# RWKV-7 attention into a SoLU block: where layer norm's mean is taken out, and a new order of the first pieces

## The chip, the cores and the metric

The kernel runs on one core of a Trainium2 chip. A core has five engines that run beside each other, each with its own stream of instructions: TensorE (PE in the profile, with its weight loads as PEld), VectorE (DVE), ScalarE (ACT), GpSimd (POOL) and SyncE (SP, which here only issues DMAs). Each engine executes its stream in the order in which the program emitted it and waits on semaphores of the others. The metric is the time of one execution on the device, in microseconds; lower is better.

## The reference

The first half is a recurrence over 768 time steps for 4 batches and 8 heads of width 40; its answers, 3072 tokens of 320 values, go into a block with a soft-max-weighted activation and a layer norm:

```python
for t in range(S):
    y[:, :, t] = np.einsum('bhd,bhde->bhe', rt, state)
    Sa = np.einsum('bhde,bhe->bhd', state, at)
    state = state * wt - outer(Sa, bt) + outer(vt, kt)
...
h = x @ w_in                                  # 3072 x 320 by 320 x 1024
e = np.exp(h - max(h));  solu = h * e / sum(e)
ln = (solu - mean(solu)) / sqrt(var(solu) + 1e-6) * g_ln
out = ln @ w_out                              # 1024 x 320
```

The weights `w_in` and `w_out` arrive as 64-bit floats, which the kernel narrows to 32 bits itself, in 13 pieces.

## The kernel before

**Chunks and slots.** Time is cut into 12 chunks of 64 steps; a piece of work called chunk i is one such chunk of two batches, so there are N = 24 of them, in two independent chains that take turns. The recurrence inside a chunk is solved with a triangular inverse of 32x32 blocks, one inversion for two chunks, in 30 dependent steps on VectorE (pieces `i0.1` to `i11.30`). The main loop runs over slots i. A slot solves chunk i of the recurrence (`S`, `R1`, `an`), prepares chunk i+1 (scores `Sk`, `Sv`, couplings `C` and `D` with their ScalarE copies `wy` and `tl`, state `Sr` with its copy `Esr`, and `K`, which reads that state), begins chunk i+5 (`w`, `a`, `b`, `k` loads, `Tc`, `Ta`, `Tb`, `N`) and runs the layer block of chunk c = i-2: the five products `H` of x with w_in, the maximum `m`, the exponential `e`, the weighing `we`, the spread `sq` with its power `rs`, then one slot later the turning `Te` with its copy `Ee`, and the products `P` and `Pr` with w_out, their scaling `Eo` and the store `So`.

**The layer norm before.** `we` (line 878, VectorE) multiplies e with h in place and gives its mean `mu`. `sq` (lines 889 to 891, ScalarE) is three instructions: the small `c2`, one pass over 128x1024 that squares (mu - 1024 e) into PSUM with a running sum, and the small `var`. `rs` (line 899, GpSimd) raises var to the power -1/2. The products with w_out use e without its mean taken out. Instead, each row of w_out (already scaled by g_ln) has the mean over all 1024 rows subtracted once, at the start: `mean_part` and `mean_more` (lines 284 and 288) build that mean with TensorE in three parts (pieces `Tmean0`, `Tmean1`, `Tmean2` in slots 1, 2 and 3), `mean_kept` (line 294) copies it with ScalarE, and `centred` (line 299, piece `centre`) subtracts it from w_out with two VectorE instructions of 128x1280. The first product `P0` reads w_out after that.

**Order.** Every piece is recorded under its name in the order of the loops, then all are emitted sorted by their place in the string `ORDER`. Names that are not in the string follow in the order of the loops. The string holds the pieces up to about slot 10, so from slot 11 on the order is the one that the loop's code gives. DMAs are issued by the engine whose queue they are given: most by SP, some loads, the inversions' blocks and x by POOL. They stand in that engine's order like its other instructions.

**Splits.** A product `H` is four matmuls of 64x512, each of which the table `SPLITS` can cut into two of 256 columns; each appears twice in the profile, since a 32-bit product takes two passes.

Of the kernel before, what the change touches and what calls it, by code (L numbers as in the profile page):

```python
# [9 lines left out]
FP32 = mybir.dt.float32  # L10
# [17 lines left out]
SPLITS = {2: (0, 0, 0, 2, 4), 24: (0, 0, 0, 0, 2)}  # L28
# [7 lines left out]
lg3 Tc3 xi3 k1 sb2 i0.1 i0.2 i0.3 i0.4 i0.5 i0.6 Tb2 Eb2 i0.7 i0.8 xe3 Tei3 Eei3 i0.9 i0.10 i0.11 i0.12 w4 N2 nt2 a3  # L36
Ta3 b3 b4 b5 i0.13 i0.14 w5 lg4 Tc4 xi4 xe4 sb3 Tb3 i0.15 i0.16 sn2 i0.17 i0.18 Tk0 cv0 Tv0 Ekv0 Tei4 K0 Ea3 Eb3 N3 a4
i0.19 L2 i0.20 i0.21 i0.22 i0.23 i0.24 i0.25 sb4 i0.26 i0.27 lg5 cr0 Tr0 nt3 Er0 i0.28 L3 Tc5 xe5 i0.29 i0.30 Eei4 sn3
a5 Tei5 Ta4 Ea4 v1 nb2 nb3 r1 ns3 Sv0 Sk0 mk0 mv0 V0 ns2 cv1 sk1 Eei5 nf3 nf2 B1 i1.1 i1.2 i1.3 x0.0 Ta5 xi5 sb5 Tb4
i1.4 i1.5 i1.6 i1.7 U0 i1.8 i1.9 i1.10 i1.11 cr1 Tv1 r2 Eb4 L4 nb4 Tk1 Ekv1 Tr1 Er1 cr2 Sk1 mk1 tu0 F0 N4 nt4 k2 i1.12  # L40
i1.13 i1.14 C0 sk2 g ns4 K1 wy0 i1.15 i1.16 uh0 i1.17 i1.18 D0 tu1 Sv1 mv1 w6 tl0 S0 lg6 Tc6 F1 Ea5 mlu0 V1 i1.19
i1.20 i1.21 k3 sk3 i1.22 i1.23 uh1 xi6 xe6 L5 nb5 clu0 R0.0 R1.0 an0 Tb5 Eb5 x0.1 Tei6 Eei6 Tg ks0 a7 v2 a6 Ta6 L6 L7
w7 Eg Tr2 N5 cv2 Tv2 Er2 b6 nt5 L8 i1.24 i1.25 i1.26 i1.27 i1.28 Tk2 Ekv2 i1.29 i1.30 lv0 C1 wy1 Sv2 ns5 D1 tl1 Ea6
nf4 nb6 Sk2 mk2 mv2 Ts2 sn5 S1 mlu1 nf5 nb7 Z2 lg7 Tc7 Es2 Sr2 ns6 Esr2 R0.1 K2 nf6 U1 xi7 sb6 clu1 nb8 R1.1 an1 sn4
l0 H0.0 ks1 ns7 nf7 xe7 Tei7 ns8 nf8 b7 Tb6 Eb6 Eei7 Ta7 Ea7 r3 cr3 B2 i2.1 i2.2 i2.3 i2.4 H0.1 i2.5 i2.6 i2.7 i2.8 V2
x0.2 H0.2 H0.3 i2.9 Tr3 Er3 uh2 N6 nt6 Ts3 Es3 Tmean0 Emean0 k4 Sr3 tu2 F2 C2 sk4 v3 cv3 w8 lg8 L11 L9 L10 H0.4 wy2
Esr3 D2 tl2 Tk3 w9 Tv3 i2.10 i2.11 i2.12 lv1 i2.13 sb7 Ekv3 Tc8 xe8 xi8 i2.14 Sv3 nb9 m0 i2.15 tu3 Tei8 b8 ns9 nf9 Tb7
# [33 lines left out]
def shape_constants():  # L81
# [19 lines left out]
def kernel(  # L101
# [1329 lines left out]
```

## Time and profile before

| | us |
|---|---|
| median of three runs | 529.92 (528.12 to 532.23) |
| the profiled execution | 526.91 |
| its span | 525.0 |
| TensorE busy | 479.6 (91%) |
| VectorE busy | 419.1 (80%) |
| ScalarE busy | 320.4 (61%) |
| GpSimd busy | 182.9 (35%) |

The span is what the profiler shows from the first instruction to the last; the execution's own time is 1.9 us longer. Everything that is worked out below is added to the profiled execution's 526.91 us and then moved to the median. A share of busy time is a mean over the start, where weights are narrowed and the first inversions run, the steady slots, and the end, where nothing is left but the layer block.

### The profile page before, as it was taken

How to read it: one execution, taken by the hardware profiler on the slowest of the kernel's cores; microseconds unless marked ns; L12 is line 12 of the kernel's file. 1: busy time of each engine (PE TensorE's matmuls, PEld its weight loads, DVE VectorE, ACT ScalarE, POOL GpSimd, SP SyncE). 2: the span in 40 equal slices, each digit the busy share in tenths (PEclk: the TensorE clock that was granted, in tenths of full speed). 3: DMA queues.
4: the chain of work that ended last, by engine and by line, in shares of the span. 5: the costliest groups of instructions: out<-in, count | busy, mean ns of one | idle time of the engine just before them, and what ended most of it. 6: DMA issues, size and time to landing. Idle time of an engine off the chain costs nothing.

```text
span 525.0 us, 28146 instructions
## 1 busy us (share of the span) xinstructions
PE 479.6 (91%) x12029; PEld 340.8 (65%) x12029; DVE 419.1 (80%) x1800; ACT 320.4 (61%) x651; POOL 182.9 (35%) x328
## 2 busy tenths in 40 slices
PE   4557587898999999999999999999999999999996
PEld 3345574766667776767776777776676767666544
DVE  5599989998998999878789879979989798443321
ACT  4646476785676654755766676666666656665433
POOL 3533246243434342543152433434252521211200
PEclk9999999999999999999999999999999999999999
DMA  9997869756666777686175675676654542421211
GB/s 161 177 187 141 181 111 217 160 119 128 140 123 142 127 164 129 149 168 135 30 147 112 114 150 119 117 150 129 126 116 90 117 111 67 96 53 28 75 41 26
DMA packets 201772, 63.97 MB, mean 122 GB/s; under 512 B 173368, under 2 KB 194592, under 8 KB 201648
## 3 DMA queue, kind: packets, MB, share of 16 engines
q1 hardware_dynamic: 188528, 41.61, 43.3%
q0 software_dynamic: 10768, 19.95, 15.5%
q8 instruction: 95, 1.56, 1.2%
q10 hardware_dynamic: 2352, 0.62, 0.6%
q14 instruction: 29, 0.24, 0.2%
HBM read 47.96 MB, written 14.16 MB: 118 GB/s over the span
## 4 chain that ended last, share of the span: by engine, by line
PE 73%; DVE 10%; DMA 6%; ACT 4%; SPq 3%; issue 3%; DVEq 0%; ACTq 0%
PE po L320 18%; PE h L320 18%; PE pyo L320 6%; PE px L320 6%; PE py L320 5%; PE ps L320 4%; PE pu L320 3%; DVE prod L562 2%; DVE uu L565 2%; PE plnT L911 2%; SPq L346 2%; PE pkv L437 2%; PE psr L320 2%; PE pa L437 2%; PE pb L437 2%
## 5 line engine op out<-in xcount | busy, mean ns | idle before, releaser
L320 PE MATMUL h<-w_in,xT 64*64 64x512 f32 (+1 forms) x1064 | 121.2, 552 | 1.7 <-issue 1.2
L320 PE MATMUL po<-w,lnT 128*64 128x320 f32 (+1 forms) x768 | 112.2, 432 | 0.0
L562 DVE TENSOR_TENSOR prod<-blk,uu 128x48 f32<-128x48 f32 (+19 forms) x576 | 93.5, 203 | 1.2
L565 DVE TENSOR_TENSOR uu<-uu,prod 128x48 f32<-128x48 f32 (+19 forms) x576 | 93.9, 203 | 0.0
L527 POOL DMA_DIRECT2D nt_dram<-nt x86 | 50.2, 591 | 101.9 <-ACT nt L515 100.7
L320 PEld LDWEIGHTS po<-w,lnT 128*64 128x64 f32 (+1 forms) x768 | 53.9, 139 | 41.6 <-issue 1.1
L320 PEld LDWEIGHTS h<-w_in,xT 64*64 64x64 f32 x1064 | 41.7, 133 | 31.4 <-issue 27.7
L899 POOL TENSOR_TENSOR rs<-var,mhalf 128x1 f32<-128x1 f32 x24 | 16.5, 686 | 120.4 <-ACT var L891 120.1
L862 DVE TENSOR_REDUCE nmax<-h 128x1 f32<-128x1024 f32 x24 | 29.3, 1220 | 31.7 <-PE h L320 31.6
L346 POOL DMA_DIRECT2D raw_r<-in_r_dram x48 | 33.2, 696 | 23.5 <-ACT r L381 22.2
L890 ACT ACTIVATE sq<-e,mu 128x1024 f32<-128x1024 f32 x24 | 26.9, 1120 | 21.4 <-DVE e L878 21.4
L870 ACT ACTIVATE e<-h,nmax 128x1024 f32<-128x1024 f32 x24 | 26.7, 1112 | 19.4 <-DVE nmax L862 19.2
L481 DVE TENSOR_TENSOR lu<-pu,cst 128x512 f32<-128x512 f32 x24 | 16.5, 686 | 24.2 <-PE pu L320 24.2
L878 DVE SCALAR_TENSOR_TENSOR e<-h,e 128x1024 f32<-128x1024 f32 x24 | 29.3, 1219 | 5.8 <-ACT e L870 5.7
L641 ACT COPY tu<-py 32x256 f32<-32x256 f32 (+1 forms) x36 | 13.2, 365 | 30.4 <-PE py L320 30.2
L830 POOL DMA_DIRECT2D x_dram<-x x24 | 18.0, 751 | 36.4 <-DVE x L821 36.3
L693 ACT COPY st<-psr 128x416 f32<-128x416 f32 (+1 forms) x44 | 14.3, 378 | 24.6 <-PE psr L320 24.5
L554 DVE SCALAR_TENSOR_TENSOR uu<-blk,uu 128x30 f32<-128x30 f32 (+3 forms) x144 | 26.8, 242 | 2.1 <-DMA blk<-nt_dram 1.5
L799 DVE TENSOR_TENSOR tot<-pyo,st 104x416 f32<-104x416 f32 x44 | 24.2, 583 | 3.5 <-PE pyo L320 3.5
L657 ACT COPY kvT<-pkv 104x1024 f32<-104x1024 f32 x24 | 24.2, 1007 | 4.4 <-PE pkv L437 4.3
L320 PE MATMUL px<-lv,psi 64*64 64x104 f32 x768 | 24.5, 265 | 2.2 <-DVE lv L481 2.2
L320 PE MATMUL pu<-x,tu 64*64 64x104 f32 x768 | 25.2, 260 | 1.0 <-ACT bT L447 0.6
(155 smaller groups left out, 1057.4 us busy)
## 6 DMA issues: line engine op xcount, KB each, us to landing
xT<-x_dram SPq DMA_DIRECT2D x48, 160.0 KB, 4.1
blk<-nt_dram POOLq DMA_DIRECT2D x22, 256.0 KB, 3.9
raw_w<-in_w_dram SPq DMA_DIRECT2D x48, 80.0 KB, 4.0
lv<-in_v_dram SPq DMA_DIRECT2D x48, 80.0 KB, 3.4
raw_r<-in_r_dram POOLq DMA_DIRECT2D x48, 80.0 KB, 3.6
out_dram<-osb SPq DMA_DIRECT2D x46, 80.0 KB, 2.6
a<-in_a_dram SPq DMA_DIRECT2D x44, 80.0 KB, 3.7
raw_k<-in_k_dram SPq DMA_DIRECT2D x42, 80.0 KB, 3.0
```

The lines of the kernel that those rows point to most:

```text
L320: nc.tensor.matmul(o, lhsT=lhsT, rhs=rhs, start=start, stop=stop, skip_group_check=True)
L346: queue.dma_start(out=x[half(p), :, 0:D], in_=ap[2 * bp + p, :, ci * C:(ci + 1) * C, :].rearrange("h t d -> t h d"))
L437: nc.tensor.transpose(out=t[0:W2, p, at + C * j:at + C * j + C], in_=x[half(p), 2 * j:2 * j + 2].rearrange("p a b -> p (a b)")[:, skip:ski ...
L527: queue.dma_start(out=blocks[n][e].rearrange("(a x h) s c -> a x s h c", a=GRP, x=2)[at, x], in_=nt[home:home + Q].rearrange("p h j c -> p ...
L554: nc.vector.scalar_tensor_tensor(out=u[:, c, j + 1:Q], in0=nb[:, j, j + 1:Q], scalar=u[:, c, j:j + 1], in1=u[:, c, j + 1:Q], op0=ALU.mult, ...
L562: nc.vector.tensor_tensor(out=ts[-1], in0=nb[:, j:j + 1, j + 1:Q].to_broadcast([P, hi - lo, m]), in1=u[:, lo:hi, j:j + 1].to_broadcast([P, ...
L565: nc.vector.tensor_tensor(out=u[:, lo:hi, j + 1:Q], in0=u[:, lo:hi, j + 1:Q], in1=x, op=ALU.add)
L657: return lambda: nc.scalar.copy(out=o[0:W2].rearrange("p b j t -> p b (j t)"), in_=t[0:W2])
L862: nc.vector.tensor_reduce(out=nmax, in_=d["h"], axis=AX.X, op=ALU.max, negate=True)
L870: nc.scalar.activation(out=e, in_=d["h"], func=AF.Exp, bias=d["nmax"], accum_out=d["esum"])
L878: nc.vector.scalar_tensor_tensor(out=d["e"], in0=d["h"], scalar=1.0 / DFF, in1=d["e"], op0=ALU.mult, op1=ALU.mult, accum_out=d["mu"])
L890: nc.scalar.activation(out=pair("A" if i == N - 2 else "h", "sq").rearrange("p a b -> p (a b)"), in_=d["e"], func=AF.Square, scale=-float( ...
```

## The change

The mean is no longer taken out of w_out's rows. The pieces `Tmean0` to `Tmean2` and `centre` go, with the functions that they called. A new piece `ce` per chunk, right after `we`, has ScalarE replace e by mu - 1024 e in place; for the last two chunks ScalarE does 512 columns and VectorE the other 512. The sign is made good in g_ln. `sq` squares this e in place, in SBUF, and needs no scale and no mu; it now stands one slot later: behind the evictions of `S` where the loop gives the order, and at places of its own where the string does. `SPLITS` of chunk 2 cuts all four matmuls in four of its five products instead of two and four in the last two. And `ORDER` is new from end to end.

```diff
-SPLITS = {2: (0, 0, 0, 2, 4), 24: (0, 0, 0, 0, 2)}
+SPLITS = {2: (0, 4, 4, 4, 4), 24: (0, 0, 0, 0, 2)}
 ORDER = """
-w0 b0 b1 w1 a0 lg0 Tc0 xi0 xe0 Tei0 sb0 Tb0 Ta0 L1 lg1 Tc1 Eei0 Ea0 v0 Eb0 xi1 xe1 N0 nt0 Tei1 Eei1 sb1 Tb1 a1 Ta1 Ea1
-L0 Eb1 N1 nt1 w2 lg2 a2 Tc2 nb0 k0 Z0 sn0 nb1 ns1 nf1 sn1q sk0 ns0 nf0 sn1 w3 xe2 b2 Z1 Ta2 xi2 B0 Tei2 Eei2 r0 Ea2
+K0 r0 r1 w0 w1 b0 b1 lg0 Tc0 xe0 Tei0 xi0 sb0 Tb0 a0 Ta0 lg1 L1 Tc1 Eei0 Ea0 Eb0 N0 xi1 xe1 nt0 sn0 Tei1 Eei1 v0 sb1
+Tb1 a1 Ta1 Eb1 Ea1 N1 nt1 a2 L0 nb0 nb1 w2 ns0 sn1q lg2 ns1 k0 k1 Tc2 xe2 sk0 Tei2 Eei2 nf1 Ta2 Ea2 a5 sk1 cv0 sn1 b2
+xi2 w3 lg3 Tc3 xe3 xi3 B0 Tei3 w4 w5 sb2 Eei3 Tb2 Eb2 N2 nt2 a3 lg4 Tc4 b3 Z0 Z1 nf0 cr0 v1 Ta3 sn2 i0.1 i0.2 L2 Tv0
...
-        mean=np.full((P, P), 2.0 ** -10),
...
-    nc.vector.memset(guard, 1e-12 / DFF)
+    nc.vector.memset(guard, 1e-12)
...
-                nc.scalar.mul(out=x, in_=pg[:, 0:NF], mul=2.0 ** y)
+                nc.scalar.mul(out=x, in_=pg[:, 0:NF], mul=-2.0 ** y)
...
-    def mean_part(t, lo, hi, start, stop=True):
...
-    def centred(mean):
-        for x in range(0, NF, NF // 2):
-            nc.vector.tensor_tensor(out=w2[:, x:x + NF // 2], in0=w2[:, x:x + NF // 2],
-                                    in1=mean.unsqueeze(1).to_broadcast([P, NF // 2, DM]), op=ALU.subtract)
...
+    def centred(i):
+        if not ok(i):
+            return
+        d = st[i]
+        e, cut = d["e"], DFF if i < N - LAG else DFF // 2
+        nc.scalar.activation(out=e[:, 0:cut], in_=e[:, 0:cut], func=AF.Identity, scale=-float(DFF), bias=d["mu"])
+        if cut < DFF:
+            nc.vector.tensor_scalar(out=e[:, cut:], in0=e[:, cut:], scalar1=-float(DFF), scalar2=d["mu"], op0=ALU.mult,
+                                    op1=ALU.add)
...
-        nc.scalar.activation(out=c2, in_=d["esum"], func=AF.Square, scale=1e-3 / DFF, bias=guard)
-        nc.scalar.activation(out=pair("A" if i == N - 2 else "h", "sq").rearrange("p a b -> p (a b)"), in_=d["e"], func=AF.Square, scale=-float(DFF), bias=d["mu"], accum_out=sq)
-        nc.scalar.activation(out=var, in_=sq, func=AF.Identity, scale=1.0 / DFF ** 3, bias=c2)
+        nc.scalar.activation(out=c2, in_=d["esum"], func=AF.Square, scale=1e-3, bias=guard)
+        nc.scalar.activation(out=d["e"], in_=d["e"], func=AF.Square, accum_out=sq)
+        nc.scalar.activation(out=var, in_=sq, func=AF.Identity, scale=1.0 / DFF, bias=c2)
...
                 evict(f"{'cm'[x]}lu{i}", box, x)
+        if ok(c - 1):
+            do(f"sq{c - 1}", spreadof, c - 1)
+            do(f"rs{c - 1}", powered, c - 1)
...
-        if i == LAG + 1:
-            mean_do("mean2", lambda: pair("A", "pmean")[:, 0], 6, NF, "mean1")
...
         if ok(c):
-            do(f"sq{c}", spreadof, c)
-            do(f"rs{c}", powered, c)
+            do(f"ce{c}", centred, c)
...
-        if i == LAG - 1:
-            mean_do("mean0", lambda tb=tb: tb()[:, 0], 0, 3)
-        if i == LAG:
-            mean_do("mean1", lambda tb=tb: tb()[:, 0], 3, 6, "mean0")
```

More of the change, by code (lines that the diff above doesn't have):

```diff
@@ L276, in evict @@
             for x, y in zip(g_cols, (0, -20, -36)):
-                nc.scalar.mul(out=x, in_=pg[:, 0:NF], mul=2.0 ** y)
+                nc.scalar.mul(out=x, in_=pg[:, 0:NF], mul=-2.0 ** y)
         return evict
-    def mean_part(t, lo, hi, start, stop=True):
-        assert len(ended) >= len(lands) + hi
-        for c in range(lo, hi):
-            nc.tensor.matmul(t[:, 0:DM], lhsT=c_("mean"), rhs=w2[:, c, :], start=start and c == lo, stop=stop and c == hi - 1)
-    def mean_more(t, lo, hi, begun=None):
-        if begun is not None:
-            nc.tensor.matmul(t[:, 0:DM], lhsT=ident, rhs=begun, start=True, stop=False)
-        mean_part(t, lo, hi, begun is None)
-        return lambda: mean_kept(t)
-    def mean_kept(t):
-        mean = two.tile([P, DM], FP32, tag="osb", name="mean", bufs=1)
-        nc.scalar.copy(out=mean, in_=t[:, 0:DM])
-        return mean
-    def centred(mean):
-        for x in range(0, NF, NF // 2):
-            nc.vector.tensor_tensor(out=w2[:, x:x + NF // 2], in0=w2[:, x:x + NF // 2],
-                                    in1=mean.unsqueeze(1).to_broadcast([P, NF // 2, DM]), op=ALU.subtract)
     def half(p):
@@ L1171 @@
     keys(7, "w")
-    mean = {}
-    def mean_do(name, t, lo, hi, begun=None):
-        evict(f"E{name}", do_pe(f"T{name}", lambda: (lambda e: lambda: mean.update({name: e()}))(
-            mean_more(t(), lo, hi, begun and mean[begun]))))
     for i in range(-1, N + LAG + 1):
@@ L1329 @@
             run(6)
-        if i == LAG + 1:
-            do("centre", lambda: centred(mean["mean2"]))
         run(7)
```

80 lines of the change are left out of this document (40 added, 40 removed).

## The prediction, made before the result was known

> **What bounds the kernel now.** I read the chain that ended last first, for the engine that the end hangs on, and then the busy time by stretches, because a mean over the span hides that the stages have different limits. The chain's shares by engine:
>
> ```profile
> PE 73%; DVE 10%; DMA 6%; ACT 4%; SPq 3%; issue 3%; DVEq 0%; ACTq 0%
> ```
>
> The chain runs through TensorE for 73% of the span. The table by stretches (busy us of each engine, with its count of instructions in brackets) says where the border lies:
>
> ```profile
> core 0: us, PE busy (x) PEld busy (x) DVE busy (x) ACT busy (x) POOL busy (x), PEclk, DMA share, GB/s
> ...
> 27.50:75.00 47.50, 32.14 (x685) 27.21 (x685) 45.06 (x253) 24.94 (x51) 14.60 (x23) 1.00 0.86 157
> 75.00:137.50 62.50, 54.55 (x1464) 39.75 (x1466) 58.98 (x222) 46.80 (x99) 30.50 (x52) 1.00 0.76 155
> 137.50:200.00 62.50, 62.32 (x1698) 44.98 (x1700) 58.50 (x277) 39.48 (x81) 24.98 (x43) 1.00 0.68 137
> 200.00:225.00 25.00, 23.84 (x681) 18.12 (x673) 22.44 (x112) 13.39 (x30) 9.18 (x16) 1.00 0.67 131
> 225.00:437.50 212.50, 210.76 (x5764) 149.32 (x5763) 182.87 (x802) 139.05 (x283) 78.22 (x131) 1.00 0.59 120
> 437.50:512.50 75.00, 74.94 (x1546) 45.19 (x1538) 33.94 (x96) 38.33 (x77) 11.41 (x19) 1.00 0.24 58
> 512.50:525.00 12.50, 7.99 (x68) 6.00 (x64) 1.92 (x3) 4.26 (x10) 0.55 (x1) 0.94 0.11 28
> ```
>
> Until 75 us VectorE is the bound (45.1 of 47.5 us; TensorE idles 15.4). From 75 to 137.5 us both are near full: VectorE idles 3.5 us, TensorE 8.0. From 137.5 us on TensorE is the bound: it idles 0.2 + 1.2 + 1.7 + 0.1 us in the next 375, and 4.5 in the last 12.5. The border is the start of the piece `S4`, the fifth group of its kind:
>
> ```profile
> 137.44 0.94 PE L320 MATMUL pu<-x,tu 64*64 64x104 f32 x32
> ```
>
> So I split the sum there: when does `S4` start, and what does each later slot lose?
>
> **What goes.** The groups of the mean, and behind them those of an inversion's steps and of one scaling of k, since they set VectorE's load (columns: busy us and mean ns of one, then idle before it):
>
> ```profile
> L284 PE MATMUL po<-w,cst 128*128 128x320 f32 x12 | 3.7, 441 | 0.0
> ...
> L284 PE MATMUL pmean<-w,cst 128*128 128x320 f32 x4 | 1.2, 432 | 0.0
> ...
> L288 PE MATMUL po<-mean,cst 128*128 128x320 f32 x2 | 0.8, 484 | 0.0
> L288 PE MATMUL pmean<-mean,cst 128*128 128x320 f32 x2 | 0.8, 484 | 0.0
> ```
>
> ```profile
> L299 DVE TENSOR_TENSOR w<-w,mean 128x1280 f32<-128x1280 f32 x2 | 2.9, 1482 | 0.0
> ```
>
> ```profile
> L565 DVE TENSOR_TENSOR uu<-uu,prod 128x48 f32<-128x48 f32 (+19 forms) x576 | 93.9, 203 | 0.0
> L562 DVE TENSOR_TENSOR prod<-blk,uu 128x48 f32<-128x48 f32 (+19 forms) x576 | 93.5, 203 | 1.2
> ...
> L430 DVE TENSOR_TENSOR kb<-raw_k,inv 128x320 f32<-128x320 f32 x24 | 11.4, 481 | 0.0
> ```
>
> TensorE loses 3.7 + 1.2 + 0.8 + 0.8 = 6.5 us, VectorE 2.9 us, all of it before `S4`. The question is whether either was on the path. I take VectorE to be it there, for it idles less than half as long as TensorE up to 137.5 us. Counting names ahead of `S4` in the two strings: inversion steps 99 before, 104 after; scalings of k 7 and 9; narrowed pieces, products `m`, `we` and evictions the same; `centre` only before. The steps that are moved are long ones, and one takes (93.9 + 93.5) / 360 = 0.5 us of the two groups; a scaling takes 11.4 / 24 = 0.5. So VectorE has 5 x 0.5 + 2 x 0.5 - 2.9 = +0.6 us more ahead of `S4`: the new string has spent what `centre` frees on steps of the inversion that used to come later. They are paid back by `S8`: ahead of it stand 172 steps against 171, without `centre`. TensorE is the bound by then.
>
> **The first inversion.** It waits for its block, which SP fetches. SP's rows, and the first inversion instruction:
>
> ```profile
> 13.10 1.31 SPq L346 DMA_DIRECT2D a<-in_a_dram  x2
> 14.45 1.72 SPq L346 DMA_DIRECT2D raw_k<-in_k_dram  x2
> 16.96 0.84 SPq L527 DMA_DIRECT2D nt_dram<-nt  x2
> ```
>
> ```profile
> 26.45 0.68 DVE L548 TENSOR_TENSOR uu<-blk,above 64x512 f32<-64x512 f32 x1 [0.71 <-DMA blk<-nt_dram]
> ```
>
> In the new order one more load (`k1`, two issues) stands on SP ahead of that store, in a place where SP has only 16.96 - 16.17 = 0.8 us free. Two issues take 1.3 us (the first row), so the store, the block behind it and `i0.1` come 0.5 us later. VectorE has other work there and idles anyway; bounds 0 and 1.3, I take +0.5.
>
> **A stall that goes.** Before `S4` VectorE waits once for long:
>
> ```profile
> 130.39 1.09 DVE L799 TENSOR_TENSOR tot<-pyo,st 104x416 f32<-104x416 f32 x2 [1.81 <-PE pyo L320]
> ```
>
> That is for `R1.3`, which TensorE does behind the last part of the mean. Without that part (1.2 + 0.8 us) TensorE is there earlier; I take the whole 1.8 away. So `S4` comes at +0.5 + 0.6 - 1.8 = **-0.7 us**. Bounds: -6.5, if TensorE alone is the path from 75 us on, and +8, if the new order makes TensorE wait as long again as it idles between 75 and 137.5 us. I am near VectorE's figure since its row is the fuller one.
>
> **Splits of chunk 2.** Sixteen cut matmuls (all four of one product, in two passes), what follows them, and eight whole ones from the chain in order of time:
>
> ```profile
> 147.55 1.08 PE L320 MATMUL h<-w_in,xT 64*64 64x256 f32 x16
> ...
> 148.56 0.43 PE L437 MATMUL pkv<-cst,v 64*104 64x64 f32 x8
> ```
>
> ```profile
> 259.39 0.86 PE h L320 x8
> ```
>
> A product cut in four takes 148.56 - 147.55 = 1.01 us in place of 0.86. Ten more of the 20 matmuls are cut, 2.5 products: 2.5 x 0.15 = **+0.4 us**, in a stretch where TensorE is full.
>
> **The pass of ScalarE.** One slot as it stands: the maximum's consumers, the turning, and ScalarE around `st`.
>
> ```profile
> 287.72 1.12 ACT L890 ACTIVATE sq<-e,mu 128x1024 f32<-128x1024 f32 x1 [0.97 <-DVE e L878]
> ...
> 289.00 0.30 ACT L891 ACTIVATE var<-sq,c 128x1 f32<-128x1 f32 x1
> ...
> 290.64 0.71 PE L911 MATMUL plnT<-cst,e 64*128 64x64 f32 x16
> ...
> 294.76 0.47 ACT L420 ACTIVATE inv<-pst 128x320 f32<-128x320 f32 x1
> 295.08 0.47 ACT L770 COPY lu<-pu 128x320 f32<-128x320 f32 x1
> ...
> 296.65 0.65 ACT L693 COPY st<-psr 128x416 f32<-128x416 f32 x2 [1.10 <-PE psr L320]
> ...
> 297.72 0.90 PE L320 MATMUL px<-st,aT 40*64 40x104 f32 x32
> ```
>
> `ce` is a pass of the size of `sq` at its place, 1.12 us, and a new thing on the way to `Te`: e is ready at 288.8 instead of 287.7. `Te` starts at 290.64, behind `Pr`, so it is covered with 1.8 us to spare, and ScalarE is even freed 0.5 us earlier than by `sq` and `var`. Cost: nothing.
>
> The moved `sq` is the piece that can cost. In slots 10 to 16 (seven, which the loop orders) it stands right behind `lu`, ahead of `st`. What it issues there: `c2`, `sq` with its read-out, `var`.
>
> ```profile
> L889 ACT ACTIVATE c<-esum,guard 128x1 f32<-128x1 f32 x24 | 7.1, 295 | 0.5
> ```
>
> From the start of `sq` to the end of `var` 289.30 - 287.72 = 1.58 us, with `c2` 1.88; neighbours overlap by 0.15 (inv ends at 295.23, lu starts at 295.08), three times here, so 1.4 to 1.9. Behind lu's end at 295.55 that gives `st` a start between 297.0 and 297.4 instead of 296.65, an end between 297.65 and 298.05, and `K` (the row px<-st) waits for it: it starts at 297.72 now. The stall is between 0 and 0.35 a slot; I take 0.13, nearer to the end with overlap, which the rows show. 7 x 0.13 = **+0.9 us**. From slot 17 on the gap ahead of `st` is longer, and `sq` fits into it but for 0.1:
>
> ```profile
> 388.65 0.65 ACT L693 COPY st<-psr 128x416 f32<-128x416 f32 x2 [1.74 <-PE psr L320]
> ```
>
> In slots 5 to 9 the string puts `sq` between other pieces, in three of them ahead of `wy`, with a product of `R1` or `K` between on TensorE; there I take nothing, and the price without that cover is in a rival. `rs` moves in POOL's queue from ahead of x's store to behind it, which only lets x go earlier.
>
> The Trainium skill, page "ScalarE: Activation LUTs", section "What ACT_TABLE_LOAD costs", has each per-partition pointer operand add about 93 ns to an activation; the new `sq` carries one less (mu), so by it `sq` would take 1.03 us, and the 0.13 would shrink to about 0.04, the sum by 0.6 us. The same page, under "The pipeline for one element", says that ScalarE reaches PSUM faster than SBUF, which speaks against the change, as `sq` now writes SBUF. No row here shows the same pass with both targets, so I keep 1.12.
>
> **The end.** Nothing covers `ce` for the last chunks. Their turnings, and the half copy that gives the price of half a pass:
>
> ```profile
> 505.50 0.57 PEld L911 LDWEIGHTS plnT<-cst,e 64*128 64x128 f32 x16 [0.49 <-DVE e L878]
> ...
> 514.41 0.08 DVE L878 DVE_READ_ACCUMULATOR e<-h,e 128x1 f32 x1
> ...
> 514.54 0.57 PEld L926 LDWEIGHTS plnT<-cst,e 64*128 64x128 f32 x16 [0.52 <-DVE e L878]
> ...
> 516.00 0.58 ACT L931 COPY lnT<-plnT 128x512 f32<-128x512 f32 x1
> ```
>
> For chunk 23 `Te` starts 0.05 us behind e; half a pass of 0.6 us and a hand-over of 0.1 come between: +0.7. For chunk 22 the queue of products hides most of it: +0.2. `sq` of chunk 23 now follows `Te` and delays the first half of the output, but not the second, which ends last. **+0.9 us**, bounds 0.6 and 1.3.
>
> **Sum.** -0.7 + 0.4 + 0.9 + 0.9 = +1.5 us: 526.91 + 1.5 = 528.4 for an execution like the profiled one. That one lies 3.0 us below the median of the three timed runs, so for the median 529.92 + 1.5 = **531.4 us**.
>
> **Rivals.** *TensorE was the path from 75 us on.* For it: the chain's 73%, and 54.55 us busy of 62.5. Against: VectorE's 58.98 there. Then the 6.5 us come out at `S4`: -6.5 + 0.4 + 0.9 + 0.9 = -4.3, 525.6 us.
>
> *The new order also fills TensorE's early waits.* It idles 15.4 us between 27.5 and 75; a third of that with the 6.5 gives -9.4, 520.5 us. Against: VectorE idles only 2.4 us there.
>
> *`sq` becomes the wait (slower).* ScalarE runs in order, so `st` in seven slots and `wy` or `st` in four of the string's (`sq1`, `sq2`, `sq3`, `sq6` stand ahead of one) wait for it. The price is 0.35 in each of the seven and the whole 1.7 in each of the four: 2.5 + 6.8 in place of 0.9, +9.9, 539.8 us. It decides once `sq` begins less than 1.7 us before TensorE finishes what `wy` or `st` copies. For it: ScalarE gains some 27 us (24 x 1.12); against: it idles 73 of the 212 us between 225 and 437.5.
>
> *The new order costs in the first slots.* The +8 bound at `S4`: +10.2, 540.1 us. For it: 900 pieces moved at once, and five more inversion steps stand ahead of `S4`.
>
> **How the numbers follow.** The forecast 0.47, TensorE as the path 0.18, the early waits filled 0.08, `sq` as the wait 0.14, the order's cost 0.13. The last two mostly come in part, between 535 and 540. The range 525 to 540 leaves out the third case and the upper parts of the last two, under 0.2. A per cent is 5.3 us, about what a measurement of this kernel can tell from no change: faster by more (below 524.6) 0.11, within 0.60, slower (above 535.2) 0.29.
>
> **What the profile after would show.** `S4` near 137 us; no rows of lines 284 to 299; rows of the new pass of about 1.1 us, 24 of them, two of 512 columns; `st` 0.4 us later behind `lu` in slots 10 to 16 with a small idle of PE ahead of px<-st, released by ACT; TensorE full from `S4` on; the last `Te` 0.7 us behind e. Wrong it would be if `S4` lies more than 3 us off, if a new releaser (ACT `sq` or `wy`) shows up for TensorE with more than 3 us, or if the first inversion starts far from 27 us.

## The result and the profile after

The changed kernel takes 531.55 us (median of 20 executions) beside 528.44 us for the kernel before on the same chip (20): a ratio of 1.0064 with a 95% interval of 1.0036 to 1.0092. Sent again with the last experiment, in a later session, it gave 531.00 beside 530.16 us, 1.0010 (0.9969 to 1.0051). Medians here are of all executions; the ratios leave out the slow ones, those over 1.5% above the fastest of their kernel. So the first session has the change 0.6 per cent slower, some 3 us, and the second has a difference of 0.8 us that can't be told from none. The profiled execution took 533.21 us, its span 531.4.

The chain that ended last, its shares by engine, in the kernel after:

```profile
PE 74%; DVE 9%; DMA 8%; ACT 4%; SPq 2%; issue 2%; DVEq 0%; ACTq 0%
```

The busy time by stretches of the kernel after (columns as in the table of before; the last borders are moved by its later end):

```profile
core 0: us, PE busy (x) PEld busy (x) DVE busy (x) ACT busy (x) POOL busy (x), PEclk, DMA share, GB/s
27.50:75.00 47.50, 32.51 (x592) 26.80 (x592) 42.56 (x226) 23.05 (x44) 19.36 (x34) 1.00 1.00 175
75.00:137.50 62.50, 53.98 (x1473) 40.75 (x1475) 59.78 (x253) 46.16 (x96) 23.60 (x41) 0.89 0.72 144
137.50:200.00 62.50, 61.03 (x1654) 44.86 (x1652) 55.82 (x252) 41.69 (x82) 24.69 (x43) 1.00 0.68 136
200.00:225.00 25.00, 24.75 (x708) 17.67 (x706) 23.24 (x115) 17.74 (x38) 5.27 (x9) 1.00 0.61 120
225.00:437.50 212.50, 208.84 (x5723) 148.43 (x5715) 182.69 (x805) 145.53 (x290) 79.51 (x137) 1.00 0.62 121
437.50:518.00 80.50, 80.32 (x1698) 49.51 (x1698) 37.48 (x115) 48.01 (x91) 13.83 (x23) 1.00 0.24 59
```

The stretch up to 75 us has lost work instead of gaining it: VectorE is busy for 42.56 us where it was 45.06, and the DMA engines are full (share 1.00, before 0.86). From 75 to 137.5 us the granted clock is 0.89. From 200 to 225 us TensorE idles 0.25 us instead of 1.16. From 225 to 437.5 us it idles 3.7 us instead of 1.7.

The groups of the new pass and of the new `sq`:

```profile
L866 ACT ACTIVATE e<-e,mu 128x1024 f32<-128x1024 f32 x22 | 25.3, 1151 | 27.1 <-DVE e L857 27.1
...
L880 ACT ACTIVATE e<-e 128x1024 f32<-128x1024 f32 x24 | 25.8, 1075 | 0.0
```

Both are near the predicted size, 1.12 us; the pass's two half pieces take 0.72 each (the row at 519.79 below), where 0.6 was predicted. The timeline of the kernel after (start, duration, then the idle time ahead with what ended it), the rows that answer to those of the prediction and the places where time went:

```profile
8.35 5.34 SPq L325 DMA_DIRECT2D a<-in_a_dram  x4
...
15.47 1.02 PE L416 MATMUL pa<-cst,a 64*104 64x64 f32 x8 [1.23 <-DMA a<-in_a_dram]
...
24.97 1.11 SPq L515 DMA_DIRECT2D blk<-nt_dram  x2
...
29.08 0.68 DVE L527 TENSOR_TENSOR uu<-blk,above 64x512 f32<-64x512 f32 x1
...
50.79 1.33 SPq L551 DMA_DIRECT2D uu_dram<-uu  x2
...
142.29 0.94 PE L299 MATMUL pu<-x,tu 64*64 64x104 f32 x32
...
259.00 0.69 PE L299 MATMUL ps<-aT,kvT 40*64 40x64 f32 x32 [1.60 <-ACT ex L435]
...
277.88 0.69 DVE L460 TENSOR_TENSOR lu<-pu,cst 128x512 f32<-128x512 f32 x1 [1.55 <-PE pu L299]
...
279.92 1.10 ACT L880 ACTIVATE e<-e 128x1024 f32<-128x1024 f32 x1
...
281.35 0.62 ACT L672 COPY st<-psr 128x416 f32<-128x416 f32 x2
...
282.06 0.98 PE L299 MATMUL px<-st,aT 40*64 40x104 f32 x31
...
519.79 0.72 ACT L866 ACTIVATE e<-e,mu 128x512 f32<-128x512 f32 x1 [1.30 <-DVE e L857]
...
520.56 0.72 PE L916 MATMUL plnT<-cst,e 64*128 64x64 f32 x16 [0.72 <-ACT e L866]
```

`S4` starts at 142.29 us, 4.85 later than before. That is the surprise; the first inversion (29.08) is 2.6 us late. To see where time is lost and won back, the table gives for each kernel that ran how far the slot's answer mask (VectorE's row lu<-pu, one in each slot) starts behind the same row of before, in us, and how far the span ends behind 525.0. One profiled execution each. "Half clock" is the time in which TensorE was granted half its clock, from one-microsecond stretches up to 240 us; before's profile has none.

| kernel | S0 | S4 | S10 | S11 | S17 | S23 | end | half clock |
|---|---|---|---|---|---|---|---|---|
| after | +4.6 | +4.9 | +1.1 | +3.2 | +3.2 | +5.0 | +6.4 | 78-89, 115-119 |
| after, again | +4.8 | +3.9 | +0.8 | +2.6 | +1.2 | +4.0 | +4.5 | 83-91 |
| r0, r1 later | +4.1 | +2.0 | -0.8 | +1.1 | +0.4 | +1.8 | +2.2 | 17-73, 109-117 |
| and L4 behind U0 | +5.0 | +1.5 | -2.4 | +1.1 | +2.7 | +3.5 | +3.9 | none |
| seam | +5.0 | +2.6 | -0.1 | +1.1 | +0.5 | +1.5 | +2.0 | 108-116 |
| start and seam | +3.8 | +1.2 | -1.7 | -0.2 | -0.7 | +1.6 | +2.0 | 17-72 |
| and v2, cv2 later | +2.9 | -0.5 | -4.0 | -2.5 | -3.6 | -3.1 | -2.6 | none |
| no ce at the end | +3.2 | +5.4 | +2.0 | +3.8 | +2.9 | +3.6 | +3.1 | 77-88, 125-129 |
| before without the mean | -0.1 | +1.8 | +2.5 | +2.5 | +3.8 | +2.7 | +2.0 | 91-98, 111-115, 125-132 |
| mean alone, rs early | +0.5 | +5.6 | +28.0 | +28.0 | +28.6 | +28.7 | +29.2 | seven stretches |
| mean alone, rs late | +1.1 | +9.3 | +10.4 | +10.4 | +11.9 | +10.2 | +10.7 | three stretches |
| order alone, rs early | +5.8 | +15.0 | +20.8 | +22.7 | +23.3 | +25.0 | +24.4 | 178-185 |
| order alone, rs late | +5.3 | +22.0 | +19.5 | +21.5 | +21.8 | +22.4 | +21.8 | four stretches |

### The profile page after: what moved, and what is told of

The parts are those of the page before. It is cut to its first block, busy times and chain, and to the rows that moved or that the text cites. A ratio compares the mean times of both kernels' runs of the same rounds, so it can differ in the third digit from the quotient of the medians.

```text
span 531.4 us, 28165 instructions
## 1 busy us (share of the span) xinstructions
PE 480.5 (90%) x12029; PEld 342.7 (64%) x12029; DVE 417.6 (79%) x1800; ACT 339.5 (64%) x672; POOL 179.5 (34%) x328
## 4 chain that ended last, share of the span: by engine, by line
PE 74%; DVE 9%; DMA 8%; ACT 4%; SPq 2%; issue 2%; DVEq 0%; ACTq 0%
PE po L299 19%; PE h L299 19%; PE pyo L299 6%; PE px L299 6%; PE py L299 5%; PE ps L299 4%; PE pu L299 3%; PE plnT L901 2%; DMA raw_b<-in_b_dram 2%; PE psr L299 2%; PE pkv L416 2%; DMA raw_w<-in_w_dram 2%; PE pa L416 2%; DMA uu_dram<-uu 1%; DVE prod L541 1%
## 5 line engine op out<-in xcount | busy, mean ns | idle before, releaser
L841 DVE TENSOR_REDUCE nmax<-h 128x1 f32<-128x1024 f32 x24 | 29.3, 1220 | 28.6 <-PE h L299 28.6
L889 POOL TENSOR_TENSOR rs<-var,mhalf 128x1 f32<-128x1 f32 x24 | 14.2, 592 | 94.3 <-ACT var L881 94.0
L866 ACT ACTIVATE e<-e,mu 128x1024 f32<-128x1024 f32 (+1 forms) x24 | 26.8, 1116 | 29.7 <-DVE e L857 29.7
L299 PE MATMUL pcum<-lw,cst 128*128 128x160 f32 x48 | 15.3, 467 | 15.9 <-ACT lw L365 15.9
L880 ACT ACTIVATE e<-e 128x1024 f32<-128x1024 f32 x24 | 25.8, 1075 | 0.0
```

The costliest lines, as they stand in the source:

```text
L299: nc.tensor.matmul(o, lhsT=lhsT, rhs=rhs, start=start, stop=stop, skip_group_check=True)
L841: nc.vector.tensor_reduce(out=nmax, in_=d["h"], axis=AX.X, op=ALU.max, negate=True)
L866: nc.scalar.activation(out=e[:, 0:cut], in_=e[:, 0:cut], func=AF.Identity, scale=-float(DFF), bias=d["mu"])
L880: nc.scalar.activation(out=d["e"], in_=d["e"], func=AF.Square, accum_out=sq)
```

## The experiments

**The loads r0 and r1 later.** In `ORDER`, from the kernel after:

```diff
-K0 r0 r1 w0 w1 b0 ...  ... Tei2 Eei2 nf1 ...  ... L3 i0.5
+K0 w0 w1 b0 ...        ... Tei2 Eei2 r0 nf1 ... ... L3 r1 i0.5
```

> The kernel after, with the loads r0 and r1 (GpSimd's queue) taken from the front of the order to where the kernel before has them, r0 behind Eei2 and r1 behind L3; nothing else is moved. Theory A, these two loads take the DMA engines from the first a, b and w loads: the first inversion starts near 27.0 us (29.08 after, 26.45 before), S0's lu at 66 instead of 69.0, and the time falls by 2 to 3 us, to a ratio of 1.001 to 1.003 to the kernel before. Rival B, the start is late for a2 and k1, which stand ahead on SyncE's queue: the inversion stays at 29, the ratio at 1.006. Rival C, the start is late for the two but the slots from 5 on absorb it: the inversion comes at 27, S4 2 us earlier, the ratio stays at 1.005 to 1.006.

Measured: 527.98 against 528.04 us, ratio 1.0029 (0.9996 to 1.0061). Timeline of this kernel:

```profile
8.04 3.65 SPq L325 DMA_DIRECT2D a<-in_a_dram  x4
...
22.61 1.11 SPq L515 DMA_DIRECT2D blk<-nt_dram  x2
...
27.18 0.68 DVE L527 TENSOR_TENSOR uu<-blk,above 64x512 f32<-64x512 f32 x1
```

The inversion comes at 27.2, as theory A has it: the four issues of a on SyncE take 3.65 us instead of 5.34, because four loads of r no longer stand ahead of them in the DMA engines, and the block's load leaves 2.4 us earlier. SyncE's queue is no cause of these 2.4 us: a2 and k1 stand where they stood, and `blk` leaves 0.5 us behind before (22.07), the figure that the prediction gave for k1; no run moves k1 alone. But S0 gains 0.5 us only (4.1 late instead of 4.6; 66 us was expected, 68.5 came), while S4 gains 2 to 3 against the two profiles of after. Against after's first ratio, 1.0064, the ratio is 1.8 us lower, near the size expected; against its second, 1.0010, nothing is gained. The trace tells the mechanism, the times can't tell the gain.

**L4 behind U0.** On top of the last edit. In the kernel after, the store `U0` of the first inverse stands on SyncE behind eight loads of `L4` and leaves at 50.79, 2.1 us behind the inversion's last step.

```diff
-... V0 L4 nf2 ... U0 nt4 ...
+... V0 nf2 ... U0 L4 nt4 ...
```

> The kernel after with r0 and r1 later, as in the first experiment, and L4 (eight loads of w_in's last part on SyncE) put behind U0, the store of the first inverse, as before has it. In the kernel after U0 leaves 2.1 us behind the inversion's last step, since L4's issues end at 50.3; before, 0.5 us. Theory A, U0 and with it S0 come 1.5 to 2 us earlier (S0 at 67 instead of 68.5), and so does every slot until VectorE is the limit, 0.5 to 2 us in the end: ratio 1.000 to 1.002. Rival B, S0 comes earlier but S2 on does not, since VectorE sets the pace from the first inversion on: ratio as with r0 and r1 alone, 1.003.

Measured: 528.87 against 527.85, ratio 1.0017 (0.9982 to 1.0051). Timeline:

```profile
46.44 1.33 SPq L551 DMA_DIRECT2D uu_dram<-uu  x2
...
54.47 1.33 SPq L325 DMA_DIRECT2D lv<-in_v_dram  x2
...
56.58 2.10 SPq L563 DMA_DIRECT2D tu<-uu_dram  x3
...
59.35 0.43 DVE L242 TENSOR_SCALAR scale<-w 128x512 int32<-128x512 int32 x1 [3.54 <-DMA lv<-in_v_dram]
...
61.35 0.46 ACT L360 COPY v<-lv 128x320 f32<-128x320 f32 x1 [4.76 <-DMA lv<-in_v_dram]
...
63.49 0.86 DVE L577 STREAM_TRANSPOSE tu<-tu 128x256 f32<-128x256 f32 x2 [0.65 <-DMA tu<-uu_dram]
...
64.08 1.08 PE L299 MATMUL py<-tu,nt 64*64 64x32 f32 x32 [5.14 <-ACT w_in L249]
```

`U0` leaves 4.4 us earlier than in the kernel after, and S0 is as late as ever. Both theories failed on S0: an earlier store of the inverse is not enough.

The row at 64.08 is the product `C0`, which `S0` hangs on. The profile names ScalarE's narrowing `ns4` (w_in, line 249) as its releaser, and `ns4` stands behind the copy `cv2`, which waits until 61.35 for the load v2. The expectation of the run with v2 and cv2 later takes that for the gate, and the rows do not bear it out. In nine profiles (before, and the eight with both the mean's change and the new order) this product starts 0.58 to 0.60 us after VectorE starts its first turning of the inverse (`tu`, line 577, here at 63.49). In the run with start and seam mended, which has the same order up to there, it starts before `ns4` does (rows below). So the gate is the turning. In the L4 run two things hold it up. VectorE's narrowing piece `nb4`, ahead of it in VectorE's order, waits 3.54 us until 59.35, now that the L4 weights it reads are issued later; the profile names the load issued next to them. The turning itself then waits 0.65 us for the load of the inverse, which left SyncE at 56.58, behind L4 and the two issues of v2.

S3 to S9 came 0.4 to 1.7 us earlier than in the last run, though S0 came later, so S0 alone is hardly what they hang on; part of it can be the clock, as the last run's profile is at half clock from 17 to 73 and from 109 to 117 us and this one is not.

**v2, cv2, cr2, ns4 and nb4 later**, on top of that and of the seam's edit (below): this run moves both suspects, ScalarE's pieces and what stands ahead of the turning (`nb4` on VectorE, v2 on SyncE).

```diff
-... U0 nt4 i1.8 nb4 r2 v2 cv2 i1.9 ... i1.13 k2 L5 k3 cr2 tu0 ... Sv1 ns4 ... uh0 C0 wy0 mk1 D0 tl0 S0
+... U0 L4 nt4 i1.8 r2 i1.9 ... i1.13 nb4 k2 L5 k3 tu0 ... Sv1 ... uh0 v2 C0 wy0 mk1 D0 tl0 cr2 ns4 cv2 S0
```

> The kernel after with r0 and r1 later, L4 behind U0, and Eei16 behind Er11 (the two changes that helped, together). Theory A, the late loads and the late ex are separate losses: S10 stands 2 us ahead of before as with the first two, the seam loses 1 us instead of 3.5, the end stays 1.4: the ratio is 0.996 to 0.999, faster than before. Rival B, the slots 10 and 11 have a limit of their own (ScalarE's queue there) that swallows any lead: the ratio stays at 1.000 to 1.002 as with the seam alone.

> As the run with the start and the seam mended, and besides the load v2 behind uh0, ScalarE's copies cv2 and cr2 and its narrowing ns4 behind tl0, VectorE's nb4 behind i1.13. In the other runs with the new order S0 stays 4 to 5 us late, even where the first inverse leaves 4 us earlier: ScalarE's copy wy0 waits behind cv2 for the load v2 (landing near 61 us). Theory A, that is S0's gate: S0's lu at 65 to 66 us instead of 69, S4 1 to 2 us earlier, the ratio 1 to 2 us below that run's. Rival B, S0 comes earlier but VectorE's load sets S2 to S4: S4 and the time as in that run.

Measured: start and seam 528.76, with v2 and cv2 later 528.20, both against 528.42; ratios 1.0017 (0.9984 to 1.0049) and 1.0025 (0.9987 to 1.0063). The product `C0` and `ns4` with start and seam mended:

```profile
62.95 1.08 PE L299 MATMUL py<-tu,nt 64*64 64x32 f32 x32 [4.91 <-DVE tu L577]
...
63.08 0.61 ACT L249 ACTIVATE w_in<-w_in 128x512 f32<-128x512 int32 x1
```

With v2 and cv2 later, the load and the turning of the inverse, and the products of S0 and S4:

```profile
54.34 2.02 SPq L563 DMA_DIRECT2D tu<-uu_dram  x3
...
60.08 0.45 DVE L577 STREAM_TRANSPOSE tu<-tu 128x256 f32<-128x256 f32 x1 [0.47 <-DMA tu<-uu_dram]
...
63.90 1.66 PE L299 MATMUL pu<-x,tu 64*64 64x104 f32 x32 [0.49 <-ACT tu L620]
...
136.99 0.94 PE L299 MATMUL pu<-x,tu 64*64 64x104 f32 x32
```

With start and seam together rival B holds by the time; by the trace S10 has a lead of 1.7 us and S11 still 0.2, so the seam takes 1.5 of it, and the end stands at +2.0. With v2 and cv2 later S0's lu stands at 67.3 us (65 to 66 were expected), 0.9 us earlier than with start and seam alone, and S4 1.6 us earlier (1 to 2 expected). The profile of start and seam is at half clock up to 72 us, though; beside the L4 run, which like this one has no half clock up to 240 us and the same pieces ahead of S10 but for the moved ones, S0 is 2.1 us and S4 2.0 us earlier. The load of the inverse leaves 2.2 us earlier than in the L4 run and the turning starts 3.4 us earlier. So the moved pieces do delay S0, but not in the way that the expectation has it: `wy0` does not wait behind `cv2` but for TensorE, 0.4 to 1.4 us in the profiles that still have `cv2` ahead of it. What `nb4` and what v2's issues cost was not separated. The profiled execution, span 522.4, is the shortest of all in the table. By the times nothing is gained: the two ratios don't differ, and neither kernel is faster than before. One execution without a stretch of half clock is not a median; what a kernel gains in such a trace is not yet a gain.

**The seam.** `ORDER` of the kernel after ends with `Eei16`, ScalarE's copy `ex`, behind six other copies; TensorE's scores of the next slot wait for it.

```diff
-... Tr11 Tei16 Tc17 Es11 tu11 Er11 xe17 xi17 S10 Eei16
+... Tr11 Tei16 Tc17 Es11 tu11 Er11 Eei16 xe17 xi17 S10
```

> The kernel after, with Eei16 (ScalarE's copy ex), which its order has as its last piece, put right behind Er11. Nothing else is moved. Theory A, the 2.06 us that the kernel after loses between S10 and S11 are ScalarE doing ex last, while TensorE's scores of the next slot wait for a later copy in its queue: S11 comes 1.5 to 2 us earlier against S10, the ratio falls from 1.006 to 1.003. Rival B, the wait moves to the next piece of ScalarE's queue (lnT, kvT): S11 gains under 0.5 us, ratio unchanged.

Measured: 528.38 against 527.85, ratio 1.0008 (0.9978 to 1.0038). The row of the scores in this kernel's timeline:

```profile
257.17 0.69 PE L299 MATMUL ps<-aT,kvT 40*64 40x64 f32 x32 [0.95 <-ACT ex L435]
```

The wait falls from 1.60 to 0.95 us, and the step from S10 to S11 loses 1.2 us against before instead of 2.1. That lies between the two theories: `ex` is close to half of the seam in this profile (with start and seam mended the step still loses 1.5). The rest stays; ScalarE is busy there without a gap from 253.2 to 259.7 us. Up to slot 10 this kernel is the kernel after, and S4 stands 2.6 us late in it, 4.9 and 3.9 in the two profiles of the other: some 1 to 2 us at S4 belong to the execution, not to the kernel.

**No ce for chunks 22 and 23.** `centred` returns at once for them.

```diff
-        if not ok(i):
+        if not ok(i) or i >= N - LAG:
             return
```

> The kernel after without the pass ce for the last two chunks (22 and 23; their mean is left in, and sq squares e as it is, so the rows of these chunks are not layer-normed). Theory A, as predicted, ce stands bare ahead of the last turnings: from S23 to the end 0.9 us less (bounds 0.6 to 1.3) than in the kernel after, 1.4 by its profile: ratio 1.004. Rival B, the end is set by the products' queue on TensorE: under 0.4 us, ratio 1.006.

Measured: 528.62 against 528.42, ratio 1.0017 (0.9987 to 1.0046). The last turning:

```profile
518.18 0.72 PE L916 MATMUL plnT<-cst,e 64*128 64x64 f32 x16
```

From S23's lu to the last turning: 490.38 to 518.18, 27.80 us; in the kernel after 491.76 to 520.56, 28.80; before 486.76 to 514.54, 27.78. The pass costs 1.0 us at the end, theory A. From the last turning to the last scaled output 5.99 us pass with and without it (5.98 before); what lies behind that, the landing of the last store, varies by itself from 3.9 to 4.9 us.

**Before without the mean.** The three parts, their copies and `centre` are dropped, nothing else.

```diff
-            mean_do("mean2", lambda: pair("A", "pmean")[:, 0], 6, NF, "mean1")
...
-            do("centre", lambda: centred(mean["mean2"]))
...
-            mean_do("mean0", lambda tb=tb: tb()[:, 0], 0, 3)
-            mean_do("mean1", lambda tb=tb: tb()[:, 0], 3, 6, "mean0")
```

> The kernel before without the mean (Tmean0 to Tmean2, their copies and centre dropped; layer norm's mean is then not taken out of the output). Theory A, as predicted, VectorE is the path ahead of S4: S4 comes 2.9 + 1.8 = 4.7 us earlier than 137.4, the time falls by 4 to 5 us, ratio 0.991. Rival B, TensorE is the path from 75 us on: 6.5 us, ratio 0.988. Rival C, what sets the slots up to 9 is the hand-over through memory of the inverses and of x (before shows such a chain between 187 and 217 us): S4 comes earlier, but S9 by less than 1.5 us, ratio 0.997 to 1.000.

Measured: 531.10 against 528.04, ratio 1.0067 (1.0031 to 1.0104). All three theories failed, since all have it faster. With 6.5 us of TensorE's and 2.9 of VectorE's work gone, S4 comes 1.8 us later. VectorE's waits between 75 and 137.5 us:

```profile
DVE tot L799 <- PE pyo L320: 5.4, 1, 5.4
```

The stall on `tot`, which the prediction took away with the mean, has grown from 1.8 to 5.4 us. TensorE was at half clock for 18 us of that stretch (91 to 98, 111 to 115, 125 to 132 us), and none of the 12 executions of this kernel had a mean clock above 0.994; of before's 91 there were 24 at 0.998 or more. So what the removal is worth at full clock no run shows. The clock is not all of it by the times: at mean clocks from 0.96 to 0.998 before has a median of 528.5 us in that session (8 executions), this kernel 531.0 (11).

**The mean's change alone**, with order and splits of before. First with `rs` right behind the moved `sq` (in this one `ce0` stands behind `Te0`, so chunk 0 is turned with its mean left in), then with `rs` at its old place ahead of `Eo`.

```diff
-... we1 an3 ... v6 sq1 Eo0 ... Es5 clu4 i3.11 ...
+... we1 an3 ... v6 ce1 Eo0 ... Es5 clu4 sq1 rs1 i3.11 ...   (first)
+... we1 an3 ... v6 ce1 Eo0 ... Es5 clu4 sq1 i3.11 ...  ... rs1 Eo1   (second)
```

> The change of the mean alone: the code after, with the order and the splits of before. ce stands where sq stood, sq and rs behind the later of S's evictions and the copy Ee, one slot later. Theory A, by the prediction's terms: S4 4.7 us earlier, then 0.9 for sq ahead of st and 0.9 at the end: 2.9 us less, ratio 0.994 to 0.996. Rival B, the kernel after is late by the mean's own change (pass and moved sq) and not by its order: S4 not later than before, but the slots 4 to 10 lose 3 to 6 us, ratio 1.004 to 1.010. Rival C, the hand-over chain of the slots 5 to 9 takes what S4 gains: only the end's 1 to 1.5 us remain, ratio 1.000 to 1.003.

> As the mean's change alone with the order and splits of before, but each rs on GpSimd stands where the kernel before has it (ahead of Eo), no longer right behind the moved sq, and ce0 stands ahead of Te0 (in the first version of it, chunk 0 was turned without its mean taken out). Theory A, the 25 us of the first version came from rs: on GpSimd the stores and the block loads of the inversions stood behind it and waited for ScalarE; then the time falls back to 1.000 to 1.008 of before, and the wait of VectorE for blk in the slots 5 to 10 (11.4 us there) falls under 3 us. Rival B, the 25 us come from ce and sq on ScalarE themselves: the ratio stays above 1.03.

Measured: the first 552.38 against 528.04, ratio 1.0474 (1.0424 to 1.0525), outside every theory; the second 535.85 against 527.85, 1.0158 (1.0100 to 1.0216). GpSimd and VectorE in the timeline of the first:

```profile
211.64 0.56 POOL L888 TENSOR_TENSOR rs<-var,mhalf 128x1 f32<-128x1 f32 x1 [12.77 <-ACT var L880]
212.24 1.08 POOL L514 DMA_DIRECT2D blk<-nt_dram  x2
...
215.82 0.68 DVE L526 TENSOR_TENSOR uu<-blk,above 64x512 f32<-64x512 f32 x1 [7.39 <-DMA blk<-nt_dram]
```

The same stretch before:

```profile
190.04 1.07 POOL L536 DMA_DIRECT2D blk<-nt_dram  x2 [3.14 <-DMA nt_dram<-nt]
194.05 0.70 POOL L899 TENSOR_TENSOR rs<-var,mhalf 128x1 f32<-128x1 f32 x1 [2.94 <-ACT var L891]
```

`rs`, half a microsecond on one column, waits 12.8 us for ScalarE's `var`, and the load of the inversion's block stands behind it in GpSimd's queue. It leaves at 212.24 instead of 190.04, and VectorE waits for it. VectorE's wait for the block between 137 and 262 us, in the first and then in the second of the two:

```profile
DVE uu L526 <- DMA blk<-nt_dram: 11.4, 2, 7.4
```

```profile
DVE uu L532 <- DMA blk<-nt_dram: 1.4, 1, 1.4
```

With `rs` back (and `ce0` ahead of `Te0`), two thirds of the loss are gone, as theory A says of the cause, though not of the remainder: it expected 1.008 at most. The other 8 us arise up to S4 (9.3 late), where beside the mean's missing parts chunk 0 has one pass more (`ce0` ahead of `Te0`, `sq0` later) and `ce1` stands for `sq1`. VectorE's waits from 75 to 262 us in the second:

```profile
DVE tot L777 <- PE pyo L298: 7.0, 3, 6.3
DVE bits L253 <- ACT scale L245: 4.8, 3, 2.3
```

VectorE waits for ScalarE's narrowing stages (4.8 us), which is in keeping with `ce0` and `sq0` in ScalarE's queue, and for `pyo`; TensorE was at half clock in part of this stretch (96-100, 109-117, 130-141 us). How much belongs to which I could not separate.

**Order and splits alone**, with the code before; the mean's pieces had to be given places, so the price is that of my places too.

```diff
-... x0.2 H0.3 ...  ... H1.0 xe9 ...  ... N8 R0.3 v6 ns12 ... H1.4 D4 ... lv2 nf12 nt8 ...  ... e1 sk8 ...
+... x0.2 Tmean0 Emean0 H0.3 ... H1.0 Tmean1 Emean1 xe9 ... N8 v6 ns12 ... H1.4 nf12 Tmean2 Emean2 R0.3 D4 ... lv2 nt8 ... e1 centre sk8 ...
```

> The order and the splits alone: the code before, with the order after (sq and rs where ce stands, Tmean0 behind x0.2, Tmean1 behind H1.0, nf12 with Tmean2 ahead of R0.3, which moves behind it, centre behind e1) and the splits after. Theory A, the order is what makes the kernel after slow: S0 4.5 us later than before as in the kernel after, S4 with the mean's work 6 to 9 us later, and 2 of the end's and seam's lost, ratio 1.010 to 1.016. Rival B, by the prediction's terms (0.5 start, 0.6 + 2.9 on VectorE, 0.4 splits): 4.4 us, ratio 1.008. Rival C, the mean's own change is what costs: ratio 1.000 to 1.003.

> As the order and splits alone with the code before, but each rs stands where the order after has it, and sq0 behind Ee0. Theory A, rs in GpSimd's queue was the 25 us: the ratio falls from 1.051 to 1.008 to 1.018, with S0 4.5 us late as in the kernel after and 6.5 us of TensorE's and 2.9 us of VectorE's work for the mean on top of it. Rival B, the mean's pieces themselves do not fit between the new order's: the ratio stays above 1.03.

Measured: 553.01 against 528.04, ratio 1.0509 (1.0451 to 1.0568), and 548.11 against 527.85, 1.0383 (1.0334 to 1.0432). The start is that of the kernel after (S0 5.8 and 5.3 late); S1 to S4, where the mean's parts stand, lose 9 and 17 us more. Rival B holds: `rs`, with `sq0` moved too, costs some 6.6 us here and is not the main cause. The order after has no room for the mean's parts at these places; whether it has some elsewhere was not tried.

**After again.**

> The kernel after once more, unchanged, to see what belongs to one execution. In its first profile the granted clock was halved at 78 to 89 us and at 115 to 119 us, and S1 stood 7.3 us late, while the kernel with only the seam mended (the same up to slot 10) had one such stretch and S1 4.4 late. Theory A, the halved stretches come and go from one execution to the next: they lie elsewhere or are missing, S1 is 4 to 5 us late and S4 2 to 3, and the ratio to before, 1.0064 the first time, is 1.003 to 1.006. Rival B, they belong to the program's order: again at 78 to 89 and 115 to 119, S1 7 late, ratio 1.006 or more.

Measured: 531.00 against 530.16, ratio 1.0010 (0.9969 to 1.0051). The stretches of half clock come and go: one from 83 to 91 us now. S0 is 4.8 late again, S1 5.0 instead of 7.3, S4 3.9. So S0's lateness is the kernel's, and a part of S1's and S4's was the execution's.

## Why the prediction was right or wrong

The sum was +1.5 us; the medians differ by +3.1 us in the first session and by +0.8 in the second. That the forecast of 531.4 us for the median lies so near the measured 531.55 is luck in two ways. The median of three that it started from, 529.92, lies 1.5 us above that of the 20, 528.44, which makes up for a sum that was 1.6 us short. And within the sum large errors cancel: in the first profile S4 is 4.9 us late where the sum has -0.7, the slots up to S10 bring back 3.7 and the step to S11 loses 2.1, for which it has no term, and S17 to S23 lose another 1.8. By the prediction's own sign, S4 more than 3 us off 137, its account of the start was wrong.

- **The first inversion, +0.5.** Measured +2.6. The step looked at the one queue that the store stands in (SyncE); its figure for k1 agrees with the run that has r0 and r1 moved: there `blk` leaves 0.5 us late. It left out GpSimd's queue: r0 and r1 at the very front load the DMA engines while a, b and w are fetched, and SyncE's own issues stretch. The inversion starts 0.7 us late then, and VectorE goes into it without a gap (the row at 27.18).
- **From the inversion to S4, +0.6 and -1.8, S4 at -0.7.** Measured +2.6 to +5.4 in the four profiles of kernels that are the same as the kernel after up to slot 10. The count of VectorE's work ahead of S4 was no price: VectorE, taken for full, stood idle for 4.9 us of the 47.5 up to 75 us, 2.4 before; 2.9 us of it were waits for DMAs, 0.5 before. S0 hung on something that the step did not name, VectorE's turning of the first inverse and the loads and pieces ahead of it. What sets S2 to S4 is hardly S0 alone, as the run with L4 suggests, and stays open. The -1.8 for `tot` is not shown either way. With the mean taken out and nothing else that wait grew to 5.4 us, but TensorE was at half clock just ahead of it (125 to 132 us). With the new order no wait at `tot` of that size is left, and VectorE idles 2.7 us from 75 to 137.5 us in the kernel after and 1.1 in the L4 run, 3.5 before.
- **Splits, +0.4.** Not seen apart. The slots 4 to 10 brought back 3.7 us in the kernel after (2.7 with the seam run): TensorE's 1.2 us of idle time from 200 to 225 us went to 0.25. The prediction had a word on the steps being paid back, but no term for this.
- **The pass, nothing in the steady slots.** Right: 22 pieces of 1.15 us and two halves of 0.72, and TensorE idles nowhere for it between S11 and S17 (3.2 late at both in the first profile).
- **`sq` ahead of `st`, +0.9.** Measured nothing: the kernel after stands 3.2 us late at S11 and at S17 (2.6 and 1.2 in its second profile). Against the slot's own lu<-pu, `st` starts at 281.35 - 277.88 = 3.47 us, where before it was 296.65 - 293.53 = 3.12: the delay of 0.35 is of the size of the prediction's. But px<-st starts 4.18 us behind that row, before 4.19: `st` now ends 0.09 us ahead of it instead of 0.42, and TensorE is at other products until then. Slots 11 to 14 are alike in this. The lower bound, 0, was the right one. On the Trainium skill's page "ScalarE: Activation LUTs", section "What ACT_TABLE_LOAD costs": one pointer fewer should have saved about 93 ns; `sq` went from 1120 to 1075 ns, 45 less, while its target moved to SBUF as well. So the trace neither confirms that figure nor shows a loss by the target. (The page has its remark on PSUM and SBUF, which the prediction cites, under "Step-by-step: what each stage is for".)
- **The end, +0.9.** Right: 1.0 us from S23 to the last turning, of which TensorE waits 0.72 for the half pass of chunk 23 (the row at 520.56).
- **Not foreseen: the seam, +2.1 and +1.8** in the two profiles of after. Where a string of the order ends and the loop's order takes over, the last copy in the string was needed first. Reading the last ten names of each string would have shown it.
- **Also not foreseen: S17 to S23, +0.5 to +2.8** in the eight profiles of kernels with both the mean's change and the new order. In the first profile of after, the products of h and psr near 426 us take 4.3 us up to px instead of 3.1, with no releaser shown. The cause stays open.

The rival that came nearest is the last, that the new order costs in the first slots. It was given 8 us at S4 and no mechanism, and took 2.6 to 5.4. The rival that `sq` becomes the wait is out in that form; but its kin, `rs` waiting ahead of the blocks on GpSimd, is what the mean's change alone runs into, some 17 us of it. The prediction saw `rs` move "from ahead of x's store to behind it" and counted only who gains. The two rivals that had TensorE's 6.5 us come out are out too: no run gained from the mean's removal.

So the change gave up 6.5 us of TensorE and 2.9 of VectorE, and bought nothing that the times show: the runs moved the first slots by where loads and single pieces stand in the engines' queues, and none got faster by taking work away. With the start or the seam mended the ratios are 1.0008 to 1.0029, none of them different from before, nor from the 1.0010 of the kernel after's second session; a version that beats both was not found.

## What to carry to other kernels

Price a moved piece on every queue it touches, and above all on the queues that also issue loads: a one-column instruction that waits in front of a block's load costs what the load's consumers wait, here some 17 us. A count of work ahead of a point is a price only if that engine never waits before the point; read its idle rows first. A releaser that one profile names is a guess: look whether the waiting row keeps its distance to it in other profiles of the same order. Where a hand-written order ends, look at who waits for its last names.

## What the runs showed of the hardware that was not expected

TensorE's granted clock drops to half in stretches of 4 to 11 us, and in some executions for some 55 us from 17 us on. Busy time by stretches (columns as above) of the kernel after, around 78 us, and then of the run with start and seam mended:

```profile
68.00:78.00 10.00, 8.45 (x174) 7.10 (x170) 8.42 (x55) 4.10 (x11) 2.32 (x4) 1.00 0.95 170
78.00:89.00 11.00, 10.41 (x264) 9.01 (x256) 9.29 (x30) 8.09 (x18) 4.35 (x8) 0.54 0.81 152
```

```profile
17.00:72.00 55.00, 32.85 (x576) 26.97 (x580) 47.11 (x232) 27.88 (x54) 25.05 (x42) 0.50 0.99 174
```

And the run with L4 behind U0, which had no such stretch:

```profile
58.00:64.00 6.00, 0.94 (x32) 0.74 (x28) 3.96 (x24) 2.62 (x5) 1.54 (x3) 1.00 0.99 165
```

In the 10 us ahead of 78 TensorE was busy for 8.45 and waited 0.7 us at most at a time, and the clock fell; in the L4 run it stood still for 5.1 us (the row at 64.08), and the clock stayed full. The Trainium skill, page "TensorE: Matmul & The Clock Gate", section "Part 1: The HAM clock gate", has the clock fall to half after an idle window of about 3.4 us. The fall at 78 us does not follow that; the one wait of 5.1 us at full clock speaks against it too, but does not decide it alone. What sets the stretches off stays open. Of before's executions that the ratios use, the 22 with a mean clock of 0.998 or more have a median of 526.9 us, and the 13 under 0.96 have 527.6; the two profiles in the table with the long early stretch and the new order have 0.941 and 0.947. So that stretch goes with little loss, as one would expect where VectorE is the bound. The 39 between, as short stretches give, have 528.9 us, 2.0 more than at full clock (0.7 to 2.9 more in each of the four sessions). That the stretches cause it was not tested.
